# Attention and Fourier mixing on one core: four products of the last second layer in two levels, and three loads and stores moved

## Chip, cores, metric

One Trainium2 chip, one of its cores. The metric is the device time of one execution in microseconds. Engines are named as in the profile: PE (matmul) and PEld (its weight loads), DVE (vector), ACT (scalar), POOL (GpSimd), SP (the engine that issues most DMAs).

## The reference, cut to what matters

```python
# q, k, v: (8, 8, 576, 64); attention without a score matrix
q_s = softmax over head_dim of q          # exp(q - max) / (sum + 1e-9)
k_s = softmax over the sequence of k
kv  = einsum('bhsd,bhse->bhde', k_s, v)
x   = einsum('bhsd,bhde->bhse', q_s, kv)  # laid out as (8, 576, 512)
# Fourier mixing and a two-layer network, fp32 (8, 576, 512) -> (8, 576, 512)
mixed = real(fft(fft(x, axis=1), axis=2))
u  = x + mixed
un = (u - mean) / sqrt(var + 1e-6)        # over the 512 columns
out = u + maximum(un @ w_ch1, 0) @ w_ch2  # 512 -> 2048 -> 512
```

The weights are given as float64 and made float32 on the chip.

## The kernel before, in words

The tokens of the eight batches are worked off in eight groups of 512: seven hold 512 tokens of one batch each, and one ("shared") holds 64 tokens of each of the eight. The order of work is group 0, then `order` 1 to 8, which take groups 1 to 6, the shared group, and group 7. For each group the layers are two matrix products.

**First layer** (`up`, matmuls in L1167): Strassen's scheme in one level, seven products in `ORDER = (1, 6, 5, 7, 2, 4, 3)`, four times over. The sums of its right side are made from the transposed, normalised tokens `unT` by `b_side` (L396 to L399). Three PSUM banks take the products: `ba` for 1 and 2, `bb` for 6, 7 and 4, `bc` for 5 and 3. Each bank has one buffer, so the next layer's first product in `bb` waits until the last sum has read it.

**Second layer** (`down`): in order 1 and in the last group seven one-level products (L1362), each 16 matmuls of 128x256. In orders 2 to 7 (`deep_down`) product 1 is one-level (L1262), and the other six are computed in a second Strassen level, two at a time (`UNITS`): 56 matmuls of 128x128 for each pair (L1283), before which `a_step` (L1238, three on DVE and one on POOL for each product) makes the sums of the left side, and after which `ends` (L1290 on DVE, L1297 and L1304 on ACT) and `into` (L1242 on POOL) add up the parts. Order 1 makes the second level's weights (`w2d`) on the way and writes them to memory. Weights stream through four places of 1 MB from a list, `self.plan`; a place that PE has `used` is loaded with the piece four further on (L447, on SP).

**Beside the layers**, during the group before, the group's tokens are made: `attention_timed` lays keys (`k_load`, `k_exp` L618 to L630, `k_turn` L642 to L655, `k_times_v` L667), own queries (`q_load` L694, `q_exp` L719 to L738, `q_turn` L746/L756, `q_times_kv` L799) and, for even batches, the queries of the shared tokens of two batches (`t_load`). `t_rows` loads the latter by four DMAs of 32 rows (L328) and a fifth that overwrites the first row of each 32 (L329). Then the Fourier steps follow, and `norm`: statistics (L1001), the root (L1005), scales (L1008, L1009), a dummy exponential that brings the exponential's table back on ACT (L1016), the four normalisations (L1030), four times four transposes on PE (L1036), copies to `unT` (L1044), and `b_side`.

**What sets the order.** Each step gets a planned time in units (one step of the plan is a piece of PE work, some 0.87 us), all steps are sorted by it, and the program is emitted in that order without a scheduler (L1541 on). Each engine runs its own instructions in this order, so one that waits holds all behind it; this holds for SP's DMA issues too. The planned times in `attention_timed`, `norm` and `down` are therefore what the change moves. In orders after 2 the next group's attention starts 7 units ahead of the next first layer (`start = -7`).

**Stores** (`store`, L1408 to L1421): one token tile in two goes straight to the output (L1412); the other, whose tokens run backwards, goes to a `mirror` in memory (L1419) and from there, head by head in pieces of 256 bytes, to the output (L1421).

Of the kernel before, what the change touches and what calls it, by code (L numbers as in the profile page):

```python
# [46 lines left out]
P = 128  # L47
# [90 lines left out]
class _Block:  # L138
    def __init__(self, ctx, tc, q, kT, v, w1, w2, ft, cd, out):
# [46 lines left out]
        for at in range(1, B + 1):  # L186
            self.base[at] = len(self.plan)
            self.plan += [self.w1s[p][:].rearrange("p a n -> p (a n)") for pair in PAIRS for p in pair]
            if self.deep(at):
                self.plan.append(self.w2s[WB_AT[1]].rearrange("p a n -> p (a n)"))  # L190
                for i in range(0, len(DEEP), 4):
                    self.plan.append(self.w2d[:, i:min(i + 4, len(DEEP)), :].rearrange("p a n -> p (a n)"))
            else:
                self.plan += [self.w2s[WB_AT[m]].rearrange("p a n -> p (a n)") for m in ORDER]
# [242 lines left out]
    def deep(self, at):  # L437

        return 1 < at < B
# [55 lines left out]
    def attention_timed(self, b, start, end):  # L495

        keys = [("k", b, r) for r in range(NR)]
        tail = [("t", b)] if b % 2 == 0 else []
        own = [("q", b, c, u) for c in range(2) for u in range(2)]
        first = start + 14 + 5 * len(tail)  # L500
        gap, steps = (end - 13 - first) / 3, []
        for i, it in enumerate(keys):
            t = start + 3.5 * i
            steps += at(t - 5.5, self.k_load(it)) + at(t, self.k_exp(it)) + at(t + 4, self.k_turn(it))
            steps += at(t + 7, self.k_times_v(it))
        for it in tail:
            t = start + 14
            steps += at(t - 6.5, self.t_load(it)) + at(t, self.q_exp(it)) + at(t + 8, self.t_turn(it))
            steps += at(21 if start < 0 else 35, self.t_fold(it))
        for i, it in enumerate(own):  # L510
            t = first + gap * i
            steps += at(t - 6.5, self.q_load(it)) + at(t, self.q_exp(it)) + at(t + 8, self.q_turn(it))
            steps += at(t + 11, self.q_times_kv(it))
        return steps + at((33 if start < 0 else 42) if tail else 22, self.t_times_kv(b))
# [184 lines left out]
    def t_load(self, it):  # L699
        _, b = it  # L700

        def load():
            if b == 0:
                q = self.at_start[3]
            else:
                q = self.work.tile([P, D], F32, tag="q", name="q", bufs=3)[:]
                self.t_rows(b, q, self.nc.sync)()
            self.live[it] = [q]

        return [(0, load)]  # L710
# [281 lines left out]
    def norm(self, g):  # L992
# [60 lines left out]
        if g == 0:  # L1053
            for some in ((0, 2), (1, 3)):
                s = slice(some[0], 4, 2)
                for i in some:
                    put(0, stats, i)
                for f in (root, scales):
                    put(0, f, s)
        else:  # L1060
            for n, i in enumerate((0, 2, 1, 3)):
                put((0, 1, 4, 5)[n], stats, i)
            s = slice(0, 4)
            put(6.5, root, s)
            put(9, scales, s)
            put(9.1, back)
        for n, i in enumerate((0, 2, 1, 3)):
            put(9.3 + 1.3 * n, normal, i)
            put(10.8 + 1.3 * n, turn, i)
            put(11.6 + 1.3 * n, laid, i)  # L1070
        put(16.5, combine)
# [142 lines left out]
    def deep_down(self, g, order):  # L1214

        nc, V, G = self.nc, self.nc.vector, self.nc.gpsimd
        base = self.base[order] + NP
# [3 lines left out]
        temps = {4: lambda i: un(i), 2: lambda i: un(3 + i), 7: self.gap, 6: dead(1), 5: dead(4), 3: dead(2)}  # L1221
# [36 lines left out]
        def single(i, q):  # L1258
            if (i, q) == (0, 0):
                bank("bb", HD)  # L1260
            for p in range(4 * q, 4 * q + 4):
                nc.tensor.matmul(box["bb"][:, i, :], lhsT=h[p][:, A_AT[1], i * P:(i + 1) * P],  # L1262
                                 rhs=self.stream[base][:, p, :], start=i == 0 and p == 0, stop=p == NP - 1,
                                 skip_group_check=True)
            if (i, q) == (1, 1):
                self.used(base)

        def one():
            nc.scalar.copy(tile(1), box["bb"][:].rearrange("p c (e n) -> p c e n", n=P))

        place = {1: "ba", 2: "ba", 6: "bb", 7: "bb", 4: "bb", 5: "bc", 3: "bc"}

        def product(unit, n, i):
            m = unit[i]
            q = DEEP.index((m, n))
            chunk = base + 1 + q // 4
# [9 lines left out]
            if q % 4 == 3 or q == len(DEEP) - 1:  # L1286
                self.used(chunk)
# [22 lines left out]
        for n in range(4):  # L1310
            put(2 * n, single, n // 2, n % 2)
        put(7.5, one)
        put(9, into, 0, 0, 1)
        n = 2 * len(ORDER)
        for i, unit in enumerate(UNITS):
            t = 8 + n * i
            for k, o in enumerate((4, 5, 2, 6)):
                for j, m in enumerate(unit):
                    early = 0 if i == 0 else t - n + 2 if i == 1 else t - n
                    put(early + (3 if i < 2 else 2) * k + j * 1.1 + 0.3, a_step, m, o)  # L1320
# [4 lines left out]
        t = 8 + n  # L1325
        put(t + 7, into, 1, 0, 4)
        put(t + 9, into, 0, 0, 2)
        t += n
        put(t + 1, sums, 6, 1)
        put(t + 3, into, 0, 1, 6)  # L1330
        put(t + 5, sums, 7, 6)
        put(t + 7, into, 1, 0, 7)
        put(t + 9, into, 1, 1, 7)
        t += n
        put(t + 1, into, 1, 1, 5)
        put(t + 2, into, 0, 1, 5)
        put(t + 4, into, 0, 1, 3)
        store(t + 3.5, 1)
        store(t + 7, 0)
        return steps  # L1340

    def down(self, g, order):
        if self.deep(order):
# [3 lines left out]
        last = order == B  # L1347
        steps, t = [], 4 * 2
        for k, m in enumerate(ORDER):
            if order == 1 and m != 1:  # L1350
# [4 lines left out]
        def product(m, bank, first):  # L1355
            n = self.base[order] + NP + ORDER.index(m)
            side = (1, 0) if last and m == 3 else (0, 1)

            def run(i, q):
# [5 lines left out]
                if (i, q) == (side[1], 1):  # L1365
                    self.used(n)
                if last and m in (4, 3) and q == 1:
                    go(sums(m == 4, m != 4, bank, i))
            return [lambda i=i, q=q: run(i, q) for i in side for q in range(2)]
# [6 lines left out]
        def sums(u, d, bank, i):  # L1376

            x = lambda: self.xs[g, u][:, i, d * HD:(d + 1) * HD]
            return [(0, lambda: V.tensor_tensor(out=x(), in0=bank()[:, i, :], in1=x(), op=ALU.add))] + at(
                0.8, self.store(g, i, u, x, d))  # L1380

        def out(u, d, store):
            def run(bank, t):
                if last and store:
                    return []
                x = lambda: self.xs[g, u][:, :, d * HD:(d + 1) * HD]
                steps = [(0, lambda: V.tensor_tensor(out=x(), in0=bank()[:], in1=x(), op=ALU.add))]
                for c in range(2):
                    if last:
                        steps += at(1 + c, self.store(g, c, u, lambda c=c: self.xs[g, u][:, c, d * HD:(d + 1) * HD], d))  # L1390
                    elif store:
                        steps += at(1 + c, self.store(g, c, u, lambda c=c: self.xpart(g, c, u)))
# [32 lines left out]
def kernel(ctx: ExitStack, tc: tile.TileContext, q, kT, v, w1, w2, ft,  # L1425
# [94 lines left out]
    n = 0  # L1520
# [16 lines left out]
    for order, g in enumerate(groups[1:], 1):  # L1537
        steps += timed(t, order, g)
        t += UP + (TWICE if blk.deep(order) else UP)
# [58 lines left out]
```

## Time and profile before

| What | us |
|---|---|
| median of 8 runs | 1119.29 |
| lowest, highest | 1115.39, 1122.70 |
| the profiled execution's own time | 1119.82 |
| its span | 1118.0 |
| PE busy | 1064.8 |
| DVE, POOL, ACT busy | 650.6, 483.0, 411.9 |
| order 2's first layer begins | 318.96 |
| order 8's (the last) first and second layer begin | 1012.74, 1060.93 |
| last matmul ends | 1111.0 |

The granted clock of PE is 0.992 over the span. Times in the text are from the span's start. A row of waits says which instruction waited for which, by engine, tile and line, with the total, the number and the longest. A row of the timeline gives start, duration, engine, line, operation and tiles, in brackets the engine's idle time before it and what ended it; consecutive equal instructions are merged. fp32 matmuls appear as two instructions each, so 16 matmuls are x32. SPq and ACTq rows are DMA issues.

### The profile page before, as it was taken

How to read it: one execution, taken by the hardware profiler on the slowest of the kernel's cores; microseconds unless marked ns; L12 is line 12 of the kernel's file. 1: busy time of each engine (PE TensorE's matmuls, PEld its weight loads, DVE VectorE, ACT ScalarE, POOL GpSimd, SP SyncE). 2: the span in 40 equal slices, each digit the busy share in tenths (PEclk: the TensorE clock that was granted, in tenths of full speed). 3: DMA queues.
4: the chain of work that ended last, by engine and by line, in shares of the span. 5: the costliest groups of instructions: out<-in, count | busy, mean ns of one | idle time of the engine just before them, and what ended most of it. 6: DMA issues, size and time to landing. Idle time of an engine off the chain costs nothing.

```text
span 1118.0 us, 16766 instructions
## 1 busy us (share of the span) xinstructions
PE 1064.8 (95%) x6240; PEld 917.9 (82%) x6240; DVE 650.6 (58%) x1295; ACT 411.9 (37%) x997; POOL 483.0 (43%) x399
## 2 busy tenths in 40 slices
PE   5789989999999999999999999999999999999997
PEld 4644446888879899889998998889988998899885
DVE  6684795664645765667655775768557743553201
ACT  6595434452225314442344224521552132132200
POOL 1064571245513545246533841465336453553320
PEclk9899999999999999999999999999999999999999
DMA  9566786546995466736674566467654664675441
GB/s 308 177 207 185 248 302 213 158 161 222 325 303 181 148 234 213 230 141 234 236 260 151 197 240 214 166 226 244 241 171 151 214 232 157 226 240 184 166 183 57
DMA packets 114482, 233.27 MB, mean 209 GB/s; under 512 B 24273, under 2 KB 76241, under 8 KB 104161
## 3 DMA queue, kind: packets, MB, share of 16 engines
q1 hardware_dynamic: 112600, 231.15, 60.6%
q10 hardware_dynamic: 1800, 1.05, 0.3%
q8 instruction: 50, 0.82, 0.3%
q14 instruction: 32, 0.25, 0.1%
HBM read 197.04 MB, written 39.32 MB: 211 GB/s over the span
## 4 chain that ended last, share of the span: by engine, by line
PE 76%; DVE 10%; ACT 4%; DMA 4%; issue 3%; POOL 2%; SPq 0%; ACTq 0%; POOLq 0%; DVEq 0%
PE bb L1167 14%; PE bc L1167 9%; PE ba L1167 9%; PE bb L1283 7%; PE bc L1283 5%; PE ba L1283 5%; PE bb L1262 3%; PE bb L1362 3%; PE acc L799 2%; PE acc L667 2%; DVE big L1238 2%; PE bc L1362 2%; PE ba L1362 2%; PE bc L1112 2%; PE acc L910 2%
## 5 line engine op out<-in xcount | busy, mean ns | idle before, releaser
L1167 PE MATMUL bb<-unT,big 128*128 128x256 f32 x768 | 185.3, 381 | 6.6 <-DVE krec L629 4.7
L389 POOL TENSOR_TENSOR big<-big 128x512 f32<-128x512 f32 (+1 forms) x38 | 46.3, 1218 | 286.4 <-ACT big L1179 285.6
L1167 PEld LDWEIGHTS bb<-unT,big 128*128 128x128 f32 x768 | 143.0, 191 | 26.7 <-DVE krec L629 6.0
L1179 ACT ACTIVATE big<-big 128x512 f32<-128x512 f32 x96 | 60.4, 629 | 182.4 <-DVE big L1178 182.1
L1167 PE MATMUL ba<-unT,big 128*128 128x256 f32 x512 | 124.1, 379 | 0.2 <-ACT unT L1044 0.2
L1167 PE MATMUL bc<-unT,big 128*128 128x256 f32 x512 | 124.1, 379 | 0.0
L1137 DVE TENSOR_TENSOR u<-bb,s 128x512 f32<-128x512 f32 x68 | 46.9, 690 | 128.0 <-PE bb L1167 88.6
L1167 PEld LDWEIGHTS ba<-unT,big 128*128 128x128 f32 x512 | 94.6, 190 | 12.3 <-ACT unT L1044 0.5
L1167 PEld LDWEIGHTS bc<-unT,big 128*128 128x128 f32 x512 | 94.5, 190 | 12.1 <-DVE big L1178 0.6
L1283 PE MATMUL bb<-big 128*128 128x128 f32 x768 | 95.8, 276 | 3.2 <-DVE u L1290 3.2
L1283 PEld LDWEIGHTS bb<-big 128*128 128x128 f32 x768 | 90.3, 192 | 4.4 <-DVE u L1290 4.4
L1242 POOL TENSOR_TENSOR x<-x,big 128x512 f32<-128x512 f32 x45 | 71.1, 1590 | 32.7 <-DVE big L1290 16.1
L725 ACT ACTIVATE q<-q,qm 128x64 f32<-128x64 f32 x240 | 64.2, 338 | 40.4 <-DVE qm L719 29.6
L1238 DVE TENSOR_TENSOR big<-big 128x512 f32<-128x512 f32 x84 | 73.8, 921 | 2.5 <-POOL big L392 2.5
L1283 PE MATMUL ba<-big 128*128 128x128 f32 x576 | 71.0, 275 | 0.0
L1283 PEld LDWEIGHTS ba<-big 128*128 128x128 f32 x576 | 68.4, 192 | 1.2
L1238 POOL TENSOR_TENSOR big<-big 128x512 f32<-128x512 f32 x24 | 37.0, 1553 | 61.9 <-DVE big L1238 61.9
L1178 DVE TENSOR_TENSOR big<-bc,u 128x512 f32<-128x512 f32 x64 | 44.0, 687 | 24.0 <-PE bc L1167 23.1
L1290 DVE TENSOR_TENSOR u<-bb,s 128x256 f32<-128x256 f32 x36 | 15.0, 418 | 69.0 <-PE bb L1283 68.7
L390 POOL TENSOR_TENSOR big<-big 128x512 f32<-128x512 f32 (+1 forms) x38 | 47.7, 1254 | 2.5
L1283 PE MATMUL bc<-big 128*128 128x128 f32 x384 | 46.8, 275 | 0.0
L383 POOL TENSOR_TENSOR big<-big 128x512 int32<-128x512 int32 x20 | 25.6, 1296 | 48.7 <-ACT ZT L925 27.6
(276 smaller groups left out, 2106.0 us busy)
## 6 DMA issues: line engine op xcount, KB each, us to landing
big<-w2d SPq DMA_DIRECT2D x60, 1024.0 KB
big<-w1s SPq DMA_DIRECT2D x64, 896.0 KB
big<-w2s SPq DMA_DIRECT2D x20, 1024.0 KB
big<-in_w_dram SPq DMA_DIRECT2D x21, 512.0 KB
w2d<-big SPq DMA_DIRECT2D x42, 256.0 KB
q<-in_q_dram SPq DMA_DIRECT2D x27, 256.0 KB
k<-in_kT_dram SPq DMA_DIRECT2D x24, 288.0 KB
v<-in_v_dram SPq DMA_DIRECT2D x24, 256.0 KB
```

Source lines behind the costliest of these rows:

```text
L389: e1.tensor_tensor(out=to(4), in0=at(2), in1=at(3), op=ALU.add)
L390: e1.tensor_tensor(out=to(2), in0=at(0), in1=at(2), op=ALU.subtract)
L725: nc.scalar.activation(q[:, h, :], q[:, h, :], ACT.Exp, bias=m[:, h:h + 1])
L1137: plus = lambda t: V.tensor_tensor(out=temp(t), in0=box["bb"][:], in1=box["s1"][:], op=ALU.add)
L1167: nc.tensor.matmul(bank()[:, i, :], lhsT=w[:, WA_AT[m], k * P:(k + 1) * P], rhs=self.unT[g][:, B_AT[m], k, :], start=first and i == 0 and ...
L1178: steps = [(0, lambda: V.tensor_tensor(out=hp(i), in0=bank()[:], in1=u()[:], op=ALU.add)), (0.8, lambda: nc.scalar.activation(hp(i), hp(i) ...
L1179: (0.8, lambda: nc.scalar.activation(hp(i), hp(i), ACT.Relu))]
L1238: e.tensor_tensor(out=to(o), in0=to(x), in1=to(y), op=op)
L1242: G.tensor_tensor(out=x, in0=x, in1=tile(m), op=ALU.add)
L1262: nc.tensor.matmul(box["bb"][:, i, :], lhsT=h[p][:, A_AT[1], i * P:(i + 1) * P], rhs=self.stream[base][:, p, :], start=i == 0 and p == 0, ...
L1283: nc.tensor.matmul(box[place[n]][:, i, :], lhsT=own(m)(A_AT[n])[:, f, :], rhs=w[:, r // 2, r % 2 * P:r % 2 * P + P], start=first and f == ...
L1362: nc.tensor.matmul(bank()[:, i, :], lhsT=h[p][:, A_AT[m], i * P:(i + 1) * P], rhs=w[:, p, :], start=first and i == 0 and p == 0, stop=p == ...
```

## The change

Five edits.

1. In the last group (order B = 8), `deep_down` replaces the one-level `down`: products 1 and 2 are one-level, then the units (7, 6) and (5, 3) in two levels, and product 4 one-level at the end. The sums of 5 and 3 go to `unT`, which is no longer used there. Products 2 and 4 are added to x by halves on DVE. The weights' list has the pieces for it: `w2s` of 1 and 2, seven of `w2d`, `w2s` of 4.
2. `t_load` allocates and loads the four row parts 12 units before the exponentials (6.5 before), and the fifth 7 units after that.
3. Own queries: their transposes and products 0.7 unit later relative to the exponentials, the gap between them slightly smaller.
4. `norm`: the dummy exponential at 16.5 (9.1 before); transposes and copies one unit later; `combine` (`b_side`) at 17.5 (16.5).
5. Order 1's stores 9 units after the sum, not 1.

Where the exponential's table is really loaded is decided by the first exponential in ACT's order. After orders 2 to 5 this is now the first key's (`k_exp`), which stands between the second and third copy to `unT`; the dummy then needs no load. After orders 1, 6 and 7 it is the dummy, between the third and fourth copy. Between third and fourth copy ACT also has the copy of product 2's sum (L1304 of before), except after order 1.

```diff
-            if self.deep(at):
-                self.plan.append(self.w2s[WB_AT[1]].rearrange("p a n -> p (a n)"))
-                for i in range(0, len(DEEP), 4):
+            one = lambda m: self.w2s[WB_AT[m]].rearrange("p a n -> p (a n)")
+            first = self.first_deep(at)
+            self.plan += [one(m) for m in (ORDER if at == 1 else (1, 2) if at == B else (1,))]
+            if at > 1:
+                for i in range(first, len(DEEP), 4):
                     self.plan.append(self.w2d[:, i:min(i + 4, len(DEEP)), :].rearrange("p a n -> p (a n)"))
-            else:
-                self.plan += [self.w2s[WB_AT[m]].rearrange("p a n -> p (a n)") for m in ORDER]
+            if at == B:
+                self.plan.append(one(4))
...
-        gap, steps = (end - 13 - first) / 3, []
+        gap, steps = (end - 13.7 - first) / 3, []
...
-            steps += at(t - 6.5, self.t_load(it)) + at(t, self.q_exp(it)) + at(t + 8, self.t_turn(it))
+            steps += at(t - 12, self.t_load(it)) + at(t, self.q_exp(it)) + at(t + 8, self.t_turn(it))
...
-            steps += at(t - 6.5, self.q_load(it)) + at(t, self.q_exp(it)) + at(t + 8, self.q_turn(it))
-            steps += at(t + 11, self.q_times_kv(it))
+            steps += at(t - 6.5, self.q_load(it)) + at(t, self.q_exp(it)) + at(t + 8.7, self.q_turn(it))
+            steps += at(t + 11.7, self.q_times_kv(it))
...
+        box = []
...
-                self.t_rows(b, q, self.nc.sync)()
+                box.append(self.t_rows(b, q, self.nc.sync))
...
-        return [(0, load)]
+        return [(0, load), (7, lambda: box and box.pop()())]
...
             put(9, scales, s)
-            put(9.1, back)
+            put(16.5, back)
         for n, i in enumerate((0, 2, 1, 3)):
             put(9.3 + 1.3 * n, normal, i)
-            put(10.8 + 1.3 * n, turn, i)
-            put(11.6 + 1.3 * n, laid, i)
-        put(16.5, combine)
+            put(11.8 + 1.3 * n, turn, i)
+            put(12.6 + 1.3 * n, laid, i)
+        put(17.5, combine)
...
+        order = (1, 2, *UNITS[1:], 4) if last else (1, *UNITS)
...
+        def add(name, u, d, i):
+            x = self.xs[g, u][:, i, d * HD:(d + 1) * HD]
+            V.tensor_tensor(out=x, in0=box[name][:, i, :], in1=x, op=ALU.add)
...
+            if unit in A_AT:
+                w = base + (i if i < 2 else 2 + (len(DEEP) - skip) // 4)
+                for k in range(4):
+                    put(t + 2 * k, single, unit, w, {1: "bb", 2: "bc", 4: "ba"}[unit], k // 2, k % 2)
...
+                for c in range(2):
+                    put(t - 4.5 + 4 * c, add, "bc" if unit == 2 else "ba", unit // 4, 0, c)
+                    half(t - 3.7 + 4 * c, c, unit // 4, 0)
...
+            early = 6 if last and t < n + 8 else 0 if t == 8 else t - n + 2 if i == 2 else t - n
...
+        if last:
+            for c in range(2):
+                half(t - 8 + 3.5 + c, c, 1, 1)
+                half(t - 8 + 6.5 + c, c, 0, 1)
...
     def down(self, g, order):
-        if self.deep(order):
+        if order > 1:
             return self.deep_down(g, order)
...
-                    elif store:
-                        steps += at(1 + c, self.store(g, c, u, lambda c=c: self.xpart(g, c, u)))
+                for c in range(2 * store):
+                    steps += at(9 + c, self.store(g, c, u, lambda c=c: self.xpart(g, c, u)))
...
-        t += UP + (TWICE if blk.deep(order) else UP)
+        t += UP + (TWICE if order > 1 else UP)
```

## The prediction

> **What bounds the kernel now.** I read the page's first section, then the waits of the tensor engine, then the timelines around the waits.
>
> ```profile
> span 1118.0 us, 16766 instructions
> PE 1064.8 (95%) x6240; PEld 917.9 (82%) x6240; DVE 650.6 (58%) x1295; ACT 411.9 (37%) x997; POOL 483.0 (43%) x399
> ```
>
> PE sets the time: 53 us of the span are without a matmul. Only two things can be gained: shorter matmul work, or PE's waits. After the opening these waits are few:
>
> ```profile
> PE tr L1036 <- ACT eo L1030: 7.5, 7, 1.5
> PE bb L1167 <- DVE krec L629: 4.7, 3, 2.6
> PE bb L1167 <- DVE u L1137: 1.8, 1, 1.8
> PE tr L746 <- DVE q L738: 1.5, 3, 0.8
> ```
>
> (Columns: total us, times, longest.) The first row is one wait in each of seven normalisations: 1.54 us in order 1, 1.24 in order 2, 0.95 in orders 3 to 7. The second is three stalls, at 329.81 (2.63, order 2), 456.71 (0.93, order 3) and 692.57 (1.19, order 5). The timeline shows what stands behind them.
>
> ```profile
> 322.45 3.90 SPq L1419 DMA_DIRECT2D mirror<-x  x1
> 326.47 0.36 SPq L577 DMA_DIRECT2D k<-in_kT_dram  x1
> ...
> 330.91 0.76 DVE L618 TENSOR_REDUCE km<-k 128x1 f32<-128x576 f32 x1 [6.45 <-DMA k<-in_kT_dram]
> ...
> 547.40 1.28 ACT L1016 ACT_TABLE_LOAD   x1
> 548.80 1.50 ACT L1030 ACTIVATE eo<-x,mv,std 128x512 f32<-128x512 f32 x2
> 549.66 0.66 PE L1036 MATMUL tr<-ident,eo 128*128 128x128 f32 x4 [0.95 <-ACT eo L1030]
> ...
> 555.24 0.59 ACT L1044 COPY unT<-tr 128x512 f32<-128x512 f32 x1
> 557.31 1.64 DVE L399 TENSOR_TENSOR unT<-unT 128x512 f32<-128x512 f32 x1
> 558.87 0.74 DVE L618 TENSOR_REDUCE km<-k 128x1 f32<-128x576 f32 x1
> 559.65 0.78 ACT L624 ACTIVATE k<-k,km 128x576 f32<-128x576 f32 x1 [2.25 <-DVE km L618]
> 560.42 0.56 ACT L646 COPY ks<-tr 128x512 f32<-128x512 f32 x1
> 561.81 1.28 PE L667 MATMUL acc<-v,ks 128*128 128x128 f32 x10
> ...
> 683.26 1.83 SPq L328 DMA_DIRECT2D q<-in_q_dram  x4
> 690.08 0.58 SPq L329 DMA_DIRECT2D q<-in_q_dram  x1
> 692.30 0.69 DVE L719 TENSOR_REDUCE qm<-q 128x8 f32<-128x512 f32 x1 [5.25 <-DMA q<-in_q_dram]
> ...
> 1110.51 2.07 SPq L1421 DMA_DIRECT2D out_dram<-mirror  x2
> ```
>
> **Part 1, the last group's second layer.** The chain of work gives the price of a product in both forms:
>
> ```profile
> 979.45 1.79 PE ba L1283 x16
> 1068.00 6.91 PE bb L1362 x32
> ```
>
> A one-level product takes 6.91 us. A two-level pair of products is seven such pieces of 1.79, 12.53 us, so 6.26 per product. Four products: 4 x (6.91 - 6.26) = 2.6 us less PE work. What it adds: 12 DVE steps (L1238, 0.92 us each) and 4 on POOL (1.55), while PE runs products 1 and 2 (13.8 us). DVE is only 20% busy there, and six of its steps are needed only for the second unit, so I cost them at nothing; without that cover the first six would cost 5.5. The half sums of products 2 and 4 each stop PE 0.52 us between halves, as rows L1379 do now: two before, two after. The weights become ten loads of 1 MB in place of seven, two of them before the layer starts; the packets of one take 3.9 us (1068.98 to 1072.85), eight of them 31 of 46 us. SP also gets a mirror store and its second half between these loads; a wait there of 3 us is covered, because a piece is asked for over 10 us before PE needs it. The end: now PE stops at 1111.0 and two mirror writes of 256-byte pieces issued together on SP end at 1116.66, the span 1.35 later. Afterwards one of them is last on SP, one having gone 35 us earlier, two going on ACT's queue. A single one should take half of the 4.67 us of both, but the (0,1) quarter is ready only after three POOL sums (3 x 1.27) behind the last two-level piece. I take 0.7 of the possible 2.3. Part 1: 3.3 us.
>
> **Part 2, shared queries in two spaced parts.** L329 overlaps the rows that L328 writes, so SP waits for their landing: 684.67 to 690.08, with v, the stores and q queued behind it, and DVE in order behind qm for 5.25 us. Only the last 1.19 of that reach PE. Now the four row transfers go before a w1s load, about 5.5 planned units (4.8 us) earlier, and the fifth 7 units after them, when they have landed. qm then comes near 689.5, which is before PE runs dry; the w1s load behind gains 256 KB (under 1 us), and no PE wait on weights exists to be lengthened. Saved: 0.93 + 1.19, and the two transposes late in its wake, 0.37 + 0.36: 2.85 us. In order 1 (b=2) nothing is seen to wait for this load. The 1.8 us row belongs to folds at 248 to 252 and stays.
>
> **Part 3, order 1's stores eight units later.** Three transfers leave the stretch before k's load, among them the mirror that stood 3.90 us in SP's queue. The load is then bounded by the transposes that free its buffer (323.8) and goes about 3.5 us earlier; PE arrives 1.5 earlier through part 4, so I count 2.4 of the 2.63. Behind the moved stores now stands the second q load, which has 4 us to spare (issued 339.9, used 347.4). The 0.7 unit (0.6 us) later transposes of queries take 0.6 of the 0.81 wait at 363.92. Part 3: 3.0 us.
>
> **Part 4, the table loaded later.** Before: the load (1.28) and its dummy (0.20) stand ahead of the normalisations, and PE waits 0.95. Without them all four eo are ready in time for the later placed transposes: +7.5 us over seven handovers. But the load doesn't go away. In the changed order of ACT, with attention following (orders 2 to 5), it stands ahead of k's exponential, both ahead of the third unT copy; the copy of product 2 (L1304) and the dummy precede the fourth. Lay out the handover at 549: PE's fourth transpose ends at 554.9; the second copy ends 552.96, load to 554.24, exponential to 555.1, third copy to 555.7, L1304 (PE half ends 555.7) to 556.3, dummy, fourth copy to 557.0. Now it ends at 555.83, so 1.17 later. Behind it stands a chain in order: DVE L396, L398, L399, L618, then ACT L624 and L646, 5.15 us (555.83 to 560.98), and PE L667 waits for L646. PE would be there 0.95 to 1.05 earlier. Today's slack before L667's weight load is 0.6. So a new wait of about 1.17 + 1.0 - 0.6 = 1.6 us arises, and PE goes on 0.55 later than now: four times -0.55. After orders 6 and 7 no keys follow; there the fourth copy ends 2.4 later (1010.4), L399 at 1013.5, and product 4's sum (L1290), which frees bank bb, at 1013.9, where PE asks for bb at 1013.2. That leaves +0.3 of 0.95 each. Order 1 has 8.6 us of matmuls between the last transposes and the next layer and gains its whole 1.54. Part 4: 1.54 + 0.6 - 2.2 = 0.0.
>
> Here a rule speaks against the change: the Trainium skill, page "ScalarE: Activation LUTs", section "What ACT_TABLE_LOAD costs", puts about 1380 ns of drain on every switch beside the load's 1283. The rows show the 1283, but the activation after it starts 0.01 us after its end and the copy before ended 0.02 before it. I take the row. By the skill the late switch would put six handovers another 1.38 back: -8.3 us, 1118.5 in all.
>
> **Sum** against the profiled execution's 1119.82 (span 1118.0 and 1.8 around it): 3.3 + 2.85 + 3.0 + 0.0 = 9.1, so 1110.7. The runs' median, 1119.29, is 0.5 below that execution: 1110.2.
>
> **Rivals.**
> - The handovers win in full: the late load is hidden and part 4 is +7.5. For it speaks the long distance from transposes to next layer (5.1 us at 673.7); against it, the 5.15 us chain with 0.6 of slack. 1102.7.
> - Parts 2 and 3 don't do what they say: the next landing or the DVE order ends the same waits. For it: PE's stalls end at DVE, which has other late inputs (k at 685.35 waited 0.49). With a third of 5.85 left: 1114.1; with nothing, 1116.0.
> - The other side: the handover takes over. If the fourth unT copy comes y later still in six handovers, the sum is 9.1 - 6y. The gain is gone at y = 1.5, and at y = 2.1 it is 1122.8. The skill's drain gives 1.38. No such pause is in the rows.
>
> **How the numbers follow.** Likeliest 0.54, 1110.2, with its own range 1106.5 to 1114 (part 4 between -3 and +3, the tail between 0 and 2). First rival 0.20, second 0.16 (two thirds of it below the bound), third 0.10, of which 0.06 past it. A measurement of this kernel can tell about 0.3%, 3.4 us. Faster: 0.54 + 0.20 + 0.10 = 0.84; same 0.10; slower 0.06. The range takes in the first rival and the second to its end: 1102.5 to 1116.
>
> **What would show it.** The last group should have 14 pieces of 1.79 us and PE's last part be 2.6 shorter; tr L1036 be gone from PE's waits; krec L629 too, save for a few tenths; and acc L667 <- ks L646 appear four times with some 1.6 us, bb L1167 twice with some 0.7. If the L667 wait is missing, I was wrong on part 4 and the time is near 1103; if it is 3 us or more, the time is back at 1119.

## The result, and the profile after

The changed kernel takes 1116.29 us (median of 19 runs, 1114.40 to 1117.56), the kernel before 1119.60 beside it (56 runs). The ratio is 0.9964, 95% interval 0.9952 to 0.9976: faster by 0.36%, some 3 to 4 us, where 9.1 were forecast. The profiled execution took 1115.72 us, with a span of 1113.9.

The page's head and the waits of PE (total us, times, longest):

```profile
span 1113.9 us, 16988 instructions
PE 1060.5 (95%) x6336; PEld 917.1 (82%) x6336; DVE 663.4 (60%) x1313; ACT 413.4 (37%) x1001; POOL 497.5 (45%) x409
```

```profile
PE acc L669 <- ACT ks L648: 13.5, 11, 3.5
...
PE bb L1171 <- DVE krec L631: 4.3, 1, 4.3
...
PE bb L1171 <- DVE u L1141: 3.3, 2, 1.8
...
PE bb L1171 <- DVE big L1304: 1.2, 2, 0.6
...
PE tr L750 <- DVE q L742: 0.7, 2, 0.4
```

Five things stand here. The seven waits tr <- eo are gone. Of the three stalls behind krec two are gone, but the third, ahead of order 2, has grown from 2.63 to 4.3. The first row holds four new waits of 1.21 (of 11; the rest belongs to the opening). The wait of 0.81 at 363.92 has become one of 1.50 on another row (u L1141, at 360.66): the sum that frees bank `bb` now stands on DVE behind the queries' steps. And the two short waits on queries (0.36, 0.37) that I had written off are still there.

To see where the time went, I cut both profiles at the starts of the layers. PE's layers, in us (first layer / second layer of each order):

| order | before | after |
|---|---|---|
| 1 | 64.45 / 58.99 | 64.14 / 57.23 |
| 2 | 66.80 / 57.31 | 69.25 / 55.86 |
| 3 | 62.92 / 55.10 | 63.63 / 53.92 |
| 4 | 60.82 / 57.02 | 62.29 / 55.85 |
| 5 | 63.18 / 55.09 | 63.63 / 55.19 |
| 6 | 60.83 / 57.14 | 62.29 / 55.96 |
| 7 | 48.35 / 49.21 | 49.23 / 48.05 |
| 8 | 48.35 / 50.08 | 49.22 / 47.61 |
| last matmul to end of span | 7.01 | 7.27 |

The opening ahead of order 1 took 195.36 before and 193.33 after; it lies anywhere between 193.3 and 195.6 in the profiles below whose opening is that of the changed kernel, so its 2.0 us can't be put down to the change. What the change did is in the table: second layers shorter by 1.2 to 1.8, first layers longer by nearly as much, and order 2's first layer 2.45 longer where I expected it some 3 shorter.

The timeline around order 2's start (start, duration, engine, line):

```profile
320.32 0.32 SPq L449 DMA_DIRECT2D big<-w1s  x1
...
321.69 0.73 SPq L579 DMA_DIRECT2D k<-in_kT_dram  x1
...
328.48 0.75 DVE L620 TENSOR_REDUCE km<-k 128x1 f32<-128x576 f32 x1 [8.12 <-DMA k<-in_kT_dram]
...
330.01 2.00 PE L1171 MATMUL bb<-unT,big 128*128 128x256 f32 x4 [4.30 <-DVE krec L631]
```

The keys' load is issued 4.8 us earlier than before (326.47), or 2.75 counted from the start of order 1 (128.36 against 131.11 us), as part 3 meant it to be. The keys came only 2.4 us earlier on the clock (328.48 against 330.91). Counted from the start of order 1 they came 0.40 earlier (135.15 against 135.55 us), while PE came 2.07 earlier (132.38 against 134.45): 2.63 + 2.07 - 0.40 = 4.30.

The stretches after this stall, with busy time of the engines and, third from the right, PE's granted clock:

```profile
330.00:331.00 1.00, 0.99 (x3) 0.81 (x4) 0.95 (x4) 0.91 (x4) 0.00 (x0) 0.56 0.02 8
331.00:332.00 1.00, 1.00 (x4) 0.81 (x3) 0.97 (x3) 0.95 (x2) 0.00 (x0) 0.50 0.00 0
332.00:333.00 1.00, 1.00 (x7) 1.00 (x6) 0.28 (x1) 0.64 (x1) 0.00 (x0) 0.50 0.00 0
333.00:334.00 1.00, 1.00 (x8) 0.97 (x7) 0.00 (x0) 0.23 (x2) 0.00 (x0) 0.74 0.00 0
```

After the stall PE runs at half its clock for 3.41 us (330.12 to 333.53), and four matmuls that take 1.03 elsewhere take 2.00. The stall costs 4.30 and then 1.7 more.

### The profile page after: what moved, and what is told of

It reads as the page before. It is cut to its first block, busy times and chain, and to the rows that moved or that the text cites. A ratio compares the mean times of both kernels' runs of the same rounds, so it can differ in the third digit from the quotient of the medians.

```text
span 1113.9 us, 16988 instructions
## 1 busy us (share of the span) xinstructions
PE 1060.5 (95%) x6336; PEld 917.1 (82%) x6336; DVE 663.4 (60%) x1313; ACT 413.4 (37%) x1001; POOL 497.5 (45%) x409
## 4 chain that ended last, share of the span: by engine, by line
PE 56%; DVE 7%; ACT 2%; issue 1%; DMA 1%; POOL 1%; SPq 0%; DVEq 0%; ACTq 0%; POOLq 0%
PE bb L1171 11%; PE bb L1297 8%; PE bc L1171 7%; PE ba L1171 7%; PE ba L1297 5%; PE bc L1297 5%; PE bb L1267 3%; DVE big L1243 2%; PE acc L669 2%; PE acc L803 1%; PE acc L951 1%; PE tr L1040 1%; PE acc L914 1%; PE acc L917 1%; DVE unT L401 1%
## 5 line engine op out<-in xcount | busy, mean ns | idle before, releaser
L1297 PE MATMUL bb<-big 128*128 128x128 f32 x848 | 105.5, 276 | 3.2 <-DVE u L1304 3.2
L1141 DVE TENSOR_TENSOR u<-bb,s 128x512 f32<-128x512 f32 x66 | 45.5, 689 | 100.0 <-PE bb L1171 87.6
L1297 PEld LDWEIGHTS bb<-big 128*128 128x128 f32 x848 | 99.6, 192 | 4.4 <-DVE u L1304 4.4
L1247 POOL TENSOR_TENSOR x<-x,big 128x512 f32<-128x512 f32 x52 | 76.6, 1483 | 35.9 <-DVE big L1304 18.4
L1243 DVE TENSOR_TENSOR big<-big 128x512 f32<-128x512 f32 x92 | 84.2, 959 | 5.9 <-POOL big L392 3.4
L1297 PE MATMUL ba<-big 128*128 128x128 f32 x640 | 79.8, 275 | 0.0
L1297 PEld LDWEIGHTS ba<-big 128*128 128x128 f32 x640 | 76.4, 192 | 1.2
L1243 POOL TENSOR_TENSOR big<-big 128x512 f32<-128x512 f32 x26 | 40.9, 1585 | 62.2 <-DVE big L1243 62.2
L1304 DVE TENSOR_TENSOR u<-bb,s 128x256 f32<-128x256 f32 x40 | 16.7, 419 | 66.2 <-PE bb L1297 48.3
L1297 PE MATMUL bc<-big 128*128 128x128 f32 x416 | 51.7, 275 | 0.0
L1267 PE MATMUL bb<-big 128*128 128x256 f32 x224 | 51.5, 381 | 0.0
```

The lines of the kernel that those rows point to most:

```text
L1141: plus = lambda t: V.tensor_tensor(out=temp(t), in0=box["bb"][:], in1=box["s1"][:], op=ALU.add)
L1243: e.tensor_tensor(out=to(o), in0=to(x), in1=to(y), op=op)
L1247: G.tensor_tensor(out=x, in0=x, in1=tile(m), op=ALU.add)
L1267: nc.tensor.matmul(box[name][:, i, :], lhsT=h[p][:, A_AT[m], i * P:(i + 1) * P], rhs=self.stream[n][:, p, :], start=i == 0 and p == 0, sto ...
L1297: nc.tensor.matmul(box[place[n]][:, i, :], lhsT=own(m)(A_AT[n])[:, f, :], rhs=w[:, r // 2, r % 2 * P:r % 2 * P + P], start=first and f == ...
```

## The experiments

Twelve kernels, each compared with the kernel before on the same chip. Four chips were used, and the kernel before takes 1118.3 to 1120.1 us on them; a difference of two medians from different chips is therefore rough by some 2 us, and where it matters I give the one by the ratios too. Line numbers move by a few lines where an edit adds or removes some.

**Part 4 undone.** The table load and the transposes go back to their old places in all seven normalisations.

```diff
-            put(16.5, back)
+            put(9.1, back)
...
-            put(11.8 + 1.3 * n, turn, i)
-            put(12.6 + 1.3 * n, laid, i)
-        put(17.5, combine)
+            put(10.8 + 1.3 * n, turn, i)
+            put(11.6 + 1.3 * n, laid, i)
+        put(16.5, combine)
```

> The changed kernel with part 4 alone undone: dummy, transposes, copies and b_side at their old times. Handover theory (the late load is paid back at the next layer's start): PE's waits for eo come back (0.95 in five orders, 1.2 and 1.5 in two), its waits for ks copies and for bank bb go; from the stages of the two traces part 4 gains 1.4 us in all, so this kernel is 1.4 us slower than the changed one, about 1117.7. Rival, the load is hidden and something else ate the gain: 7.5 us slower, about 1124. Rival, part 4 only harms: faster than the changed kernel, near 1114.

Measured: 1111.21, ratio 0.9944 (0.9925 to 0.9964), 5.1 below the changed kernel by the medians, 2.2 by the ratios, 5.6 in the profiles from the start of order 1. The waits tr <- eo are back (1.54, 0.95 ...), yet order 2's first layer takes 64.04 in place of 69.25, and PE's stall there is short:

```profile
330.52 1.13 PE L1171 MATMUL bb<-unT,big 128*128 128x256 f32 x4 [0.74 <-DVE krec L631]
```

So part 4 doesn't come to nothing, as my sum had it: it costs. The question is whether it costs in order 1 or in the later handovers.

**The old places in order 1 alone** (`g == 2` is the group that order 1 normalises):

```diff
-            put(16.5, back)
+            put(9.1 if g == 2 else 16.5, back)
...
-            put(11.8 + 1.3 * n, turn, i)
-            put(12.6 + 1.3 * n, laid, i)
-        put(17.5, combine)
+            put(11.8 - (g == 2) + 1.3 * n, turn, i)
+            put(12.6 - (g == 2) + 1.3 * n, laid, i)
+        put(17.5 - (g == 2), combine)
```

> Changed kernel with the old place of the table load and of the transposes in order 1's normalisation alone (the six later ones keep the new place). Theory: it is there that the change lost what part 3 should have brought. PE comes 1.76 us later, but the weights' sums' writes and behind them the keys land some 1.8 us earlier in relation; the stall falls from 4.30 to about 0.7 and the lowered clock behind it (1.6) goes: about 1112.5. Rival: the gain of the kernel with all seven old places (5.1 us) came from the later handovers; then the stall stays above 2.5 and the time at 1116.

Measured: 1111.19, ratio 0.9924 (0.9900 to 0.9949). Order 1's second layer is 59.00 again (1.77 longer than after), order 2's first layer 63.23 (6.02 shorter), and no wait behind krec is left. The median equals that of the kernel above (1111.21), and by the ratios this one is ahead: what part 4 costs, it costs in order 1, and the later handovers are too small to be told by the total. The keys' load is issued at nearly the same place (128.24 us after order 1's start; 128.36 in after), yet the keys come 2.59 earlier (132.56 against 135.15). What goes ahead of them is earlier, not their issue:

```profile
326.51 0.75 DVE L620 TENSOR_REDUCE km<-k 128x1 f32<-128x576 f32 x1 [3.77 <-DMA k<-in_kT_dram]
```

**Part 3's place.** Order 1's stores at their old planned time, and 8 units later still:

```diff
-                    steps += at(9 + c, self.store(g, c, u, lambda c=c: self.xpart(g, c, u)))
+                    steps += at(1 + c, self.store(g, c, u, lambda c=c: self.xpart(g, c, u)))
```

> The changed kernel with order 1's stores at their old places, ahead of the keys in SP's queue. Theory of the bytes (the keys land when all that was given to the DMA queues ahead of them has gone through): three more transfers of 256 KB and one in small pieces stand ahead, the keys land some 3 us later and PE's wait in order 2 grows from 4.3 to 6 to 7 us: 1118.5 to 1119. Theory of the issue (the prediction's): the same direction, 2.4 us. Rival, the wait is set by the weights' writes alone: no change, 1116.3.

Measured: 1117.88, ratio 0.9995 (0.9982 to 1.0009); the stall is 5.19, not the 6 to 7 expected, and order 2's first layer 71.48, 2.2 longer than after. The keys' load is issued 4.0 us later than in after (132.33 against 128.36 from order 1's start), and the keys come only 0.9 later.

```diff
-                    steps += at(9 + c, self.store(g, c, u, lambda c=c: self.xpart(g, c, u)))
+                    steps += at(17 + c, self.store(g, c, u, lambda c=c: self.xpart(g, c, u)))
```

> The changed kernel with order 1's stores eight units later still, so that the mirror and output stores that stand directly ahead of the keys go behind them. The keys' issue is then the same (it waits for the transposes that free the buffer and the weights' load). Theory of the bytes: 512 KB fewer ahead, the keys land 1.6 to 2.6 us earlier, PE's wait in order 2 is 1.7 to 2.7 instead of 4.3: about 1114.2. Theory of the issue: no change, 1116.3.

Measured: 1110.99, ratio 0.9943 (0.9923 to 0.9964); the stall is 3.60, where 1.7 to 2.7 was expected, the first layer 68.53. So the stores ahead of the keys do matter, 0.9 and 0.7 us of stall each way, less than I expected. Against the changed kernel the medians differ by 5.3 us, the ratios by 2.4 and the profiles, from order 1's start, by 2.7: 0.7 of that is the layer, 1.27 a wait in order 5 that this profile doesn't have (below), and 0.7 the time after the last matmul.

**The keys ahead of a weight load.** The load at 320.32 frees nothing that the keys need; it stands ahead of them and moves 0.9 MB.

```diff
-                if (i, q) == (1, 1):
+                if (i, q) == (1, 1) and m != 3:
                     self.used(n)
...
+        steps.append((UP + 1.6, lambda: self.used(self.base[order] + NP + ORDER.index(3))))
```

> Changed kernel with one first-layer weight load of 0.9 MB in order 1 put behind the keys' load on SP in place of ahead of it. Theory A, the keys land late because of the bytes that stand ahead of them in the transfers: they land 3 to 4 us earlier, the stall of 4.30 at order 2's start falls to 1 or less, TensorE's clock isn't lowered after it (another 1.6): about 1111. Theory B, the keys are bound by the release of their buffer (the transposes, 323.8): they can't come before 326, stall 2 to 3, about 1115. Against both: the weights moved back could now be late for PE, which would show as a wait on the stream's weights in order 2.

Measured: 1110.42, ratio 0.9916 (0.9891 to 0.9941). The keys' maximum starts at 325.34, 131.42 after order 1's start (135.15 in after), and the stall is 0.57; order 2's first layer takes 63.86. No wait on weights appears.

```profile
325.34 0.75 DVE L620 TENSOR_REDUCE km<-k 128x1 f32<-128x576 f32 x1 [4.39 <-DMA k<-in_kT_dram]
```

The keys' load is issued 1.4 us earlier than in after (127.00 from order 1's start), and the keys come 3.7 earlier. So what holds the keys is what lies ahead of them in the transfers, not the transposes that free their buffer, at which I had put the bound.

**The same edit on the kernel before**, to price the stall without anything of the change:

```diff
-                if (i, q) == (side[1], 1):
+                if (i, q) == (side[1], 1) and (m != 3 or last):
                     self.used(n)
...
+        if order == 1:
+            steps.append((UP + 1.6, lambda: self.used(self.base[order] + NP + ORDER.index(3))))
```

> The kernel before, with nothing of the change, and one edit: in order 1 one first-layer weight load of 0.9 MB goes behind the keys on SP. It tests what a stall at order 2's start costs. Theory: the stall of 2.63 falls to 1 or less, and the half clock behind it (0.5 for some 3.3 us, in the profile of before 66.80 us of first layer where 63.4 are explained by matmuls at full clock and waits) goes too: order 2's first layer 62.5 to 63.4, 3.4 to 4.3 us less, 1115 to 1116. Rival, only the wait itself is won: 1.6 to 2.6 us, first layer 64.2 or more. Against both: two stores of order 1 still stand between the weights and the keys here, the mirror with 3.90 us on SP; if they bound the keys, the stall stays above 2.

Measured: 1114.93, ratio 0.9950 (0.9933 to 0.9967). The stall of 2.63 is gone, and order 2's first layer goes from 66.80 to 62.29: 4.51 us for a wait of 2.63. This one moved load is worth about as much as the whole change.

**Why the keys come late: the rounds of the weight sums.** Before order 2, SP works in rounds: it loads a piece of w1s (L449), then issues seven writes of summed weights to w2d, then waits until the writes before have landed and loads the next. The keys stand behind the last round. These are the loads that begin and end the third round, of before, after, and the kernel with order 1 as before:

```profile
296.14 0.33 SPq L447 DMA_DIRECT2D big<-w1s  x1
...
304.09 0.32 SPq L447 DMA_DIRECT2D big<-w1s  x1
```

```profile
293.98 0.33 SPq L449 DMA_DIRECT2D big<-w1s  x1
...
303.55 0.32 SPq L449 DMA_DIRECT2D big<-w1s  x1
```

```profile
294.69 0.33 SPq L449 DMA_DIRECT2D big<-w1s  x1
...
302.82 0.32 SPq L449 DMA_DIRECT2D big<-w1s  x1
```

7.95, 9.57 and 8.13 us. The sums on DVE that feed these writes stand where they stood: in the kernel with all seven old places they come 2.31 to 2.40 us later than in after from 286 to 312, and order 1 begins 2.32 later; SP issues the same writes. In all eight kernels with the late table in order 1 and the same opening this round takes 9.41 to 11.33 us, in the four with the early one (before, its edit above, and the two with old places) 7.78 to 8.57. What differs in the transfers is one packet. The queues' view gives packets, MB and the packets' time as a share of 16 engines; a packet counts whole in the stretch in which it starts, so a share can pass 100%. First the third round of after (294.0 to 303.6), then that of before (296.2 to 304.1):

```profile
q1 hardware_dynamic: 3694, 3.36, 106.8%
q8 instruction: 1, 0.02, 0.6%
```

```profile
q1 hardware_dynamic: 3414, 2.83, 109.1%
```

A packet of 16 KB that carries instructions falls into the round (at 300.18, 0.95 us long). It is PE's: the page counts 50 packets on q8, and PE has 12,672 matmuls and weight loads, 253 for each packet. In all eight kernels with the late table it lies inside the round; in the four with the early one it falls after it.

Two kernels move PE's packets and leave every transfer of data in its place, by matmuls in the opening whose output nobody reads:

```diff
+    def idle(self, bank, at):
...
+        for _ in range(at.get(n, 0)):
+            self.nc.tensor.matmul(bank, lhsT=self.ident[:], rhs=self.ident[:], start=True, stop=True)
...
             pk = self.acc((P, P))
+            self.idle(pk, {0: 8, 6: 8})
...
             px = self.acc((P, D))
+            self.idle(px[:, 0:P], {2: 5, 4: 5, 5: 6, 6: 16, 7: 6})
```

> The changed kernel with 54 more matmuls, whose output nobody reads, in the opening (some 216 instructions of TensorE[...]; they may cost the opening 2 to 6 us, so read from the start of order 1's first layer). The packet then falls about 4 us later, in the fourth round of writes, as in the kernels with the early table, while the table stays late. Theory: the third round takes 8.0 to 8.6 us in place of 9.57, keys land 1 to 2 us sooner against order 1, the stall of 4.30 becomes 2 to 3. Rival, the late table's copies or the earlier transposes themselves hold the writes: the round stays at 9.4 or more and the stall at 4.3.

Measured: 1118.94, ratio 1.0001 (0.9985 to 1.0017), with an opening 5.3 us longer (198.65), which is the price of the extra matmuls. The packet is at 308.60, and the third round has none:

```profile
q1 hardware_dynamic: 3486, 2.87, 109.9%
```

The weight loads that begin and end the round, and the keys' maximum:

```profile
299.27 0.33 SPq L457 DMA_DIRECT2D big<-w1s  x1
...
307.26 0.32 SPq L457 DMA_DIRECT2D big<-w1s  x1
...
331.79 0.75 DVE L628 TENSOR_REDUCE km<-k 128x1 f32<-128x576 f32 x1 [6.12 <-DMA k<-in_kT_dram]
```

The round takes 7.99 us (299.27 to 307.26), the keys come 133.14 us after order 1's start in place of 135.15, and the stall is 2.30 in place of 4.30. The late table and the late transposes are all still there. The packet now falls into the fourth round, and there it costs nothing: 7.64 us, where the late-table kernels without it take 7.82 to 8.26. So the packet lengthens the third round, and not any round.

```diff
+            self.idle(px[:, 0:P], {6: 10})
```

(on the kernel with the old places in order 1 alone)

> The kernel with order 1's table early (its predecessor here: keys in time, order 2's first layer 63.2 us) and 10 more matmuls, whose output nobody reads, in a pause of TensorE near 138 us. They are some 40 instructions of TensorE, so the 16 KB packet that carries its instructions by DMA comes that much sooner, about 4 us: it moves from the fourth round of weight-sum writes (where the writes wait for DVE anyway) into the third, at about 300 to 301 us. Theory, that packet holds one of 16 DMA engines for 0.95 us and the round ends with the slowest: the third round takes 9.4 us or more in place of 8.1, the keys land 1 to 2 us later, a stall of 0.5 to 2 appears ahead of order 2, time 1112 to 1114. Rival, the place of the packet is a by-product: the round stays at 8.1 to 8.6, no stall, 1111.2.

Measured: 1114.43, ratio 0.9964 (0.9951 to 0.9977), against 1111.19 for its predecessor. A stall of 1.71 appears where there was none, and the keys come 134.32 us after order 1's start in place of 132.56. But the packet went further than meant: to 295.97, 0.30 us before the third round begins, not into its end. The round takes 9.00 us, and the whole from there to the last load 1.2 us longer than in its predecessor. This supports the same cause, less directly than the kernel with the later packet.

**Part 2 undone.**

```diff
-            steps += at(t - 12, self.t_load(it)) + at(t, self.q_exp(it)) + at(t + 8, self.t_turn(it))
+            steps += at(t - 6.5, self.t_load(it)) + at(t, self.q_exp(it)) + at(t + 8, self.t_turn(it))
...
-        return [(0, load), (7, lambda: box and box.pop()())]
+        return [(0, load), (0, lambda: box and box.pop()())]
```

> Changed kernel with the shared queries' load again in one piece (part 2 undone, all else kept). My forecast's part 2: the two stalls behind krec in orders 3 and 5 (0.93 and 1.19) and the two late transposes (0.37 and 0.36) come back, 2.85 us, so about 1119.1 beside the changed kernel's 1116.3. Rival, from the changed kernel's own rows: the two transposes' waits (0.36, 0.37) are still there, so they never hung on this load; and the keys' wait of 1.21 ahead of each stall makes PE later, so part of the stalls is hidden: 1 to 2 us, about 1117.8.

Measured: 1118.04, ratio 0.9982 (0.9968 to 0.9995), 1.75 above the changed kernel by the medians, 2.0 by the ratios. PE's waits in orders 3 to 5, of this kernel:

```profile
PE bb L1171 <- DVE krec L631: 2.0, 2, 1.2
PE tr L750 <- DVE q L742: 0.7, 2, 0.4
```

The two stalls come back (1.23 and 0.81), the two waits on queries are as long with the load in one piece as in two. They never hung on it.

**Part 1 undone** (the last group's second layer in one level again, with its old stores; the edit puts back the removed lines of the diff and leaves order 1's stores as after).

```diff
-            self.plan += [one(m) for m in (ORDER if at == 1 else (1, 2) if at == B else (1,))]
-            if at > 1:
+            self.plan += [one(m) for m in (ORDER if at in (1, B) else (1,))]
+            if 1 < at < B:
...
-        if order > 1:
+        if 1 < order < B:
             return self.deep_down(g, order)
```

> The changed kernel with the last group's second layer in one level as before. By the price of the pieces (6.91 against 6.26 us a product) the second layer takes 2.5 us more and the rest nothing: 1118.6. If the 3 MB more of weights or the DVE steps had cost something elsewhere, the difference would be smaller; if the tail after the last matmul differs by the place of the mirror writes, it is seen there (7.0 against 7.3 us).

Measured: 1116.91, ratio 0.9990 (0.9976 to 1.0004). The last layer takes 50.08 in place of 47.61, 2.47 longer. But the end after the last matmul is 5.18 us in this profile, in place of 6.35 to 7.28 in the eleven with part 1. That is no price of part 1: the two other kernels with a one-level last group issue the same last stores and need 7.01 (before) and 7.37 us. The medians (0.6 us apart) and the ratios (0.26%, 2.9 us) leave open how much of the 2.47 reaches the total.

**The waits behind ks.** The handover at 549 after the change, on ACT, DVE and PE:

```profile
550.48 1.28 ACT L626 ACT_TABLE_LOAD   x1
551.78 0.78 ACT L626 ACTIVATE k<-k,km 128x576 f32<-128x576 f32 x1
...
553.81 0.58 ACT L1048 COPY unT<-tr 128x512 f32<-128x512 f32 x1
...
555.87 1.64 DVE L401 TENSOR_TENSOR unT<-unT 128x512 f32<-128x512 f32 x1
557.43 0.74 DVE L620 TENSOR_REDUCE km<-k 128x1 f32<-128x576 f32 x1
...
558.98 0.56 ACT L648 COPY ks<-tr 128x512 f32<-128x512 f32 x1
...
559.59 1.38 PE L669 MATMUL acc<-v,ks 128*128 128x128 f32 x10 [1.21 <-ACT ks L648]
```

The keys' maximum (L620) stands in DVE's order behind the three sums of the transposes, the last of which takes 1.64. This kernel plans it ahead of them:

```diff
-            steps += at(t - 5.5, self.k_load(it)) + at(t, self.k_exp(it)) + at(t + 4, self.k_turn(it))
+            top, *rest = self.k_exp(it)
+            early = 1.5 if start < 0 and i == 1 else 0
+            steps += at(t - 5.5, self.k_load(it)) + at(t - early, [top]) + at(t, rest) + at(t + 4, self.k_turn(it))
```

> Changed kernel with the maximum over the second keys (km) planned 1.5 units earlier in the handovers, so that it stands ahead of the last two sums of the norm's transposes on DVE. Theory: the four waits acc <- ks of 1.21 come only from km standing in order behind those sums; they shrink to 0.2 or less, four times 1 us: about 1112. Rival: the sums (which PE's next layer and the next weight sums need) are then late instead, or ks was bound by the exponential: the waits move, no gain or a loss, 1116 to 1118.

Measured: 1112.33, ratio 0.9930 (0.9903 to 0.9956), although the stall ahead of order 2 happens to be 6.04 in its profile. The four waits shrink to one of 0.2, and the first layers of orders 3 to 6 are shorter by 0.97, 1.08, 1.15 and 1.48.

**Three edits together**: the keys ahead of the weight load, the maximum ahead of the sums, and no dummy exponential after orders 6 and 7, where no keys follow.

```diff
-            put(16.5, back)
+            if g < B - 1:
+                put(16.5, back)
```

> Three edits on the changed kernel together: one weight load behind the keys in order 1, the second keys' maximum ahead of the last sums in the handovers, and no table load with its dummy after orders 6 and 7, where no exponential follows. If the causes are separate their gains add: 5.9 (to 1110.4 alone), 4 x 1.1 to 1.2 from the four waits behind ks, and up to 0.6 twice from the waits for bank bb: about 1105, PE's waits acc <- ks and bb <- krec both under 0.6. If they share a wait, 1108 or more.

Measured: 1103.58, ratio 0.9858 (0.9838 to 0.9879): faster than both kernels, by 1.4% and 1.1%. Its waits behind krec and ks from order 1 on:

```profile
PE acc L671 <- ACT ks L650: 1.7, 2, 1.5
...
PE bb L1174 <- DVE krec L633: 0.3, 1, 0.3
```

The waits for bank bb at 914.45 and 1011.72 are gone too, and the first layers of orders 7 and 8 are 48.35 again in place of 49.23. Of the waits behind ks one, of 1.5 in order 3, is longer than expected.

## Why the prediction was wrong

**Part 3 is the step that failed.** I wrote that the load "is then bounded by the transposes that free its buffer (323.8) and goes about 3.5 us earlier", and counted 2.4 of the stall's 2.63. The sum itself is off: 3.5 for the keys less the 1.5 by which PE comes earlier leaves 2.0. Measured from the start of order 1, the issue went 2.75 earlier, but the keys gained 0.40. An issue is no landing: ahead of the keys lay a weight load of 0.9 MB and stores, and ahead of those a chain of rounds that ends each time with the landing of writes. With the 0.9 MB moved behind them the keys gained another 3.7. I followed the queue of issues on SP and not the bytes. The second half of part 3, 0.6 of the wait at 363.92, failed too: a wait of 1.50 (0.69 more) stands there.

The experiments say where the keys' gain went. With part 4 undone and the stores moved, the keys come 2.99 earlier than before (old places in order 1) or 2.20 (in all), and the stall is 0 or 0.74: on its own, moving the stores does nearly what part 3 asked of it. What my sum had not is what part 4 does in order 1. It brings PE to the stall 1.8 earlier, and it brings the packet into the third round, which holds the keys back to 135.15 from order 1's start. With the packet alone moved away they come at 133.14, between the two kernels with the old places (132.56 and 133.35), and the stall of 2.30 that is left is about what PE's earlier arrival makes of it.

**Part 4 was right in its own terms and wrong in what it did to part 3.** Order 1's 1.54 was 1.76. The new wait in orders 2 to 5 was 1.6 in the forecast and 1.21 in the profile; a handover nets a loss of about 0.3 there (first layer +1.5, second -1.2) where I had 0.55, and a gain of 0.3 after orders 6 and 7, as forecast. The waits for bb, forecast at some 0.7, are 0.61. The drain of 1.38 that speaks against the change in the forecast is not there: the load at 550.48 follows the copy before it at once, and the exponential starts 0.02 after its end. But PE's earlier arrival at a stall that the keys end is worth nothing, and I counted it as 1.54 won. Undoing part 4 in order 1 alone gives 1111.19. That this is close to the forecast of 1110.2 is in part luck: some 1.7 of it is the clock, which no part of the forecast had.

**What no step had: the price of the clock.** The half clock stands in the profile of before, too:

```profile
333.00:334.00 1.00, 1.00 (x4) 0.79 (x3) 0.95 (x5) 0.91 (x3) 0.00 (x0) 0.50 0.00 0
334.00:335.00 1.00, 1.00 (x6) 0.91 (x5) 0.71 (x1) 0.58 (x2) 0.00 (x0) 0.50 0.00 0
```

I priced the stall at its wait. It costs about 1.7 us more (half of 3.41), and so the one term that went wrong was larger than I had it on both sides: removed, 4.5 instead of 2.6; kept, no gain at all.

**Part 2** was 2.85 in the forecast and 1.75 by the medians, 2.0 by the ratios: the two stalls (2.12 forecast, 2.04 when the load is put back) are right, the transposes "late in its wake" (0.73) are not. **Part 1**: 2.47 of PE's 2.6. The tail's 0.7 can't be told: it is 0.26 longer in this profile, but 6.35 to 7.28 over the eleven kernels with part 1 and 5.18, 7.01 and 7.37 in the three without. **In order 5** the profile of after has a wait of 1.02 that before has not (bb <- unT L1243, at 751.97, DVE held by a key load); it stands in three of the kernels with the change and not in the others, and its cause is open.

By the table: part 1 -2.47 and, in the tail, +0.26; part 2 -1.8 (what orders 3 and 5 gained beside orders 4 and 6); order 2's first layer +2.45, order 1's first and second -0.31 and -1.76; the six other handovers +0.3; the wait in order 5 +1.27. That is -2.1, and the spans differ by 2.05 without the opening. The runs differ by 3.3 (medians) to 4.0 us (ratio); one profile of each kernel does not place the rest. Of the rivals, "parts 2 and 3 don't do what they say" (1114.1 to 1116.0) was nearest; it had the mechanism, that the next landing ends the same wait, for part 3. The one on the other side did not come: the handover's new wait stayed below the forecast.

The Trainium skill, page "TensorE: Matmul & The Clock Gate", section "What's actually happening", gives a free-running window of about 3.4 us: after an idle one the clock halves, after a busy one it is back. The length agrees (3.41 us at 0.5). But the window before need not be idle: before the change PE was still busy 0.82 us of it and the clock halved all the same, and the measurement decides. Page "Runtime: NRT & Kernel Launch", section "Instruction fetch mechanics", says that instructions come in 16 KiB blocks of 256 over a DMA queue and that the cost is mostly hidden. The size and the rate agree; the cost was hidden from PE but not from the writes under way in the third round.

## What to carry over

Follow a late input to its landing, not to its issue: write down what lies ahead of it in bytes, and what has to land before those bytes are even asked for. When one edit makes the waiting engine come earlier and another makes the input come earlier, add them on one clock, counted from a common point; the earlier arrival at a wait that another ends is worth nothing. Price a stall of PE by its wait and by the clock in the stretches after it.

## What was not expected of the hardware

- **What a stall of PE costs beyond its length depends on where it falls.** In each of the 14 profiles the times at which the granted clock changes lie whole multiples of 3.41 us apart (before: 32.03, 38.85, 144.67, 148.08, 332.40, 335.81; after: 330.12, 333.53). I cut the time around order 2's start into these windows. After a window at full clock in which PE was busy 1.09 us or less, the next one ran at half clock; after one with 1.69 or more it did not. The stall of 3.60 (stores later still) put 2.32 into one window and cost the clock; the one of 2.30 (packet later) was split over two and cost none. The first number behind the length is PE's busy time, the third from the right the clock; two windows of the former, three of the latter:

```profile
327.97:331.38 3.41, 1.09 (x6) 0.98 (x7) 2.54 (x7) 1.60 (x4) 0.00 (x0) 1.00 0.40 143
331.38:334.79 3.41, 3.41 (x15) 3.14 (x14) 1.15 (x3) 1.72 (x4) 0.00 (x0) 0.50 0.04 13
```

```profile
328.42:331.83 3.41, 2.60 (x16) 1.99 (x15) 0.04 (x1) 0.00 (x0) 0.00 (x0) 1.00 0.97 346
331.83:335.25 3.42, 1.93 (x13) 1.83 (x14) 3.31 (x9) 2.45 (x5) 0.00 (x0) 1.00 0.55 189
335.25:338.66 3.41, 3.41 (x21) 3.05 (x21) 1.93 (x7) 1.99 (x5) 0.00 (x0) 1.00 0.52 166
```

  Order 2's first layer less its waits is 61.5 to 62.0 us in the seven profiles without half clock there (stalls of 0 to 2.30), and 63.4 to 64.8 in the seven with it (2.63, 3.60, 4.30, 4.94, 5.03, 5.19, 6.04). In the two longest the stall reached 0.63 and 1.39 us into the window at half clock, and the next was at half clock too: 6.83 us in all. Where between 1.09 and 1.69 the border lies is open; elsewhere in these profiles it is not sharp (half clock after 1.83 us, full clock after 1.42), so this is no fixed threshold.
- **One packet of instructions, 16 KB and 0.95 us, can lengthen a round of transfers by some 1.5 us.** It is 0.6% of the work in the third round of after, yet the round with it takes 9.57 us, and 7.99 when the packet is moved. In one profile the round took 11.33. In the fourth round the same packet cost nothing. Why it can cost so much is not shown: the trace does not say on which engine a packet lay.
- **An edit that moves no transfer moved this one.** With transposes that wait for ACT the packet came 2.7 to 3.4 us after the first of them (before, its edit above, and the two kernels with old places), in after 0.7 us before it. Why is open.
